# Turning the attention sinks by a float32r product, folding the older key block into the current one, and a new order of work

## The chip, the cores and the metric

The kernel runs on one core of a Trainium2 chip. The metric is the device time of one execution in microseconds (us); three runs of the kernel before took 260.81, 260.99 and 261.70 us, median 260.99. The engines of the core work side by side, each through its own list of instructions in order: TensorE (PE in the profile, its weight loads PEld), VectorE (DVE), ScalarE (ACT), GpSimd (POOL) and SyncE (SP), which issues most of the DMAs.

## The reference

Two layers, in float32, for B = 4, H = 8 heads, S = 768 positions, head width D = 64. First attention with a window and sinks, then a gated layer with a causal convolution of five taps:

```
scores = (q @ k.T) / sqrt(64)
keep   = (key < n_sink) | (0 <= query - key < window)      # n_sink 4, window 128
a      = exp(where(keep, scores, -1e9) - max);  a = a / (sum(a) + 1e-9)
x      = (a @ v)  laid out as [4, 768, 512]
gate   = 1 / (1 + exp(-conv5(x)));  out = ((gate * (x @ w_val)) @ w_out)
```

w_val, w_out and conv_w come as 64-bit numbers and are turned into pairs of float32r tiles in the kernel.

## The kernel before, in words

There are 24 steps s = (b, p, qd): batch b, a third p of the positions (256 queries), and a half qd of the head pairs. Two consecutive steps (qd = 0 and 1) make one block m = s // 2 of the second layer. `ORDER` is the whole plan: a list of 849 events, and each event (`s0.7` is `scores` of step 7, group 0) issues its instructions when its turn comes (line 685), so the order on every engine is written out by hand. All buffers rotate; a load or a product that needs a buffer in use waits for it.

The events of one step, with the line that issues their main instruction:

- `kq`, `vv` (234, 245): SyncE loads of k, q and v. `sv` (255) readies the sink rows of v on ScalarE and GpSimd.
- `s0`, `s1` (`scores`, 376): queries against keys, in float32. A query chunk c of 128 sees three key blocks of 64 (n = 200 columns with four sink columns behind each of the first two). Per group 16 products of a 64 x 32 tile and 168 columns, each as two instructions (L396). Window 128 over blocks of 64 means that for query r in its block the oldest key block counts at columns above r and the current one up to r, so one block can be folded into the other by a predicated copy (L401, VectorE): before, the current block is written over the oldest one where `low` is set, and the 132 columns [oldest, sinks, middle] are used. Then a maximum (L405), or for p = 0 mask and minimum in one (L410), where `mask` removes what lies ahead of the sequence.
- `e0`, `e1` (414): exp with its sum on ScalarE. `rec` (425): the reciprocal. `norm` (430): GpSimd multiplies the window part into `wx` (L436) and the sink part into `skb`, in three copies: the value (L440), its remainder (L444) and its rounding to float32r (L443).
- `tx` (449): 16 transposes of `wx` on TensorE; `px` (483) and `py` (491) mask and copy them into `wt`.
- `sk` (`sinks_t`, 462): the transpose of `skb` on TensorE (L464); `ts` (466): masks and rounds it into `skt`.
- `vl` (507): probabilities times values, float32 on 64 x 64 tiles (L518); `si` (522): the sinks' part, float32r (L526).
- `xc`, `xh`, `hd`, `xl` (531 to 550): x as float32 and as a high and a low float32r part. `c4`, `c0`, `c1` (552 to 562): the five taps. `th` (564): the gate, by tanh.
- per block, `v0` to `v3` (572): x @ w_val, 12 float32r products of 128 x 128 with 256 columns each (L581); `g`, `h`, `l` (597 to 610): gate times value and its two parts; `o0` to `o3` (612): times w_out, 6 products of 512 columns each (L634; the last block's second half as 12 of 256, L630). `t`, `d` (647, 658): copy and store.

The weights are decoded at the start (events `wv..`, `wo..`); there `woc` makes `wo_f` on GpSimd (L161) and `woe` uses it on TensorE (L184). `masks`, `signs`, `leads` and `blanks` (276 to 338) fill constants: `lead` holds what step 0 adds to its scores by a product, `plus` is the identity in float32r, `blanks` clears `skb`.

Of the kernel before, what the change touches and what calls it, by code (L numbers as in the profile page):

```python
# [42 lines left out]
s0.4 xh.1 vv.2 woe.1 c0.1 e1.3 rec.3 woa.3 th.0 vv.5 e0.4 xl.1 v0.0 v1.0 c1.1 y0.0 wob.3 woa.2 norm.3 g0.0  # L43
wod.3 h0.0 vl.2 wob.2 th.1 s1.4 e1.4 l0.0 v2.0 v3.0 woe.3 woe.2 y1.0 g1.0 vv.6 tx.3 px.3 si.2 xc.2 hd.2 wof.1
h1.0 s0.6 o2.0 o0.0 rec.4 xh.2 py.3 c4.2 c0.2 l1.0 wof.2 s0.5 c1.2 s1.6 kq.7 wod.2 e0.6 wof.3 o1.0 t0.0 o3.0
norm.4 sk.3 e0.5 vv.3 ts.3 t1.0 xl.2 vl.3 si.3 xh.3 xc.3 hd.3 xl.3 c4.3 sk.4 th.2 s1.5 ts.4 tx.4 sv.6 px.4
e1.5 kq.8 c0.3 scalars d0.0 py.4 rec.5 v0.1 v1.1 y0.1 c1.3 e1.6 rec.6 v2.1 norm.5 g0.1 th.3 h0.1 v3.1 vv.4
y1.1 vl.4 tx.5 d1.0 kq.9 si.4 g1.1 l0.1 px.5 s1.8 sk.5 hd.4 xc.4 ts.5 o0.1 h1.1 c4.4 o2.1 xh.4 c0.4 warm_up
c1.4 py.5 l1.1 e1.8 o3.1 t1.1 s0.7 s1.7 vl.5 xl.4 norm.6 kq.10 tx.6 e0.7 si.5 sk.6 py.6 px.6 ts.6 xc.5 xh.5
o1.1 hd.5 e1.7 xl.5 s0.9 rec.7 t0.1 s0.8 v0.2 c4.5 c0.5 v1.2 th.4 kq.12 g0.2 v2.2 c1.5 e0.9 norm.7 e0.8 rec.8  # L50
sk.7 h0.2 v3.2 l0.2 norm.8 tx.7 ts.7 th.5 g1.2 vl.6 py.7 si.6 px.7 hd.6 h1.2 xc.6 c4.6 l1.2 xh.6 xl.6 s1.9
s1.10 vv.7 c0.6 c1.6 o2.2 o0.2 vv.8 sv.7 e1.9 e1.10 o3.2 tx.8 rec.9 px.8 s0.12 vl.7 norm.9 kq.18 py.8 t1.2
si.7 xc.7 c4.7 s0.10 tx.9 d0.1 sk.8 hd.7 xh.7 xl.7 ts.8 th.6 c0.7 kq.11 e0.12 e0.10 o1.2 d1.2 v0.3 px.9 c1.7
vv.9 v1.3 g0.3 s1.12 py.9 t0.2 s0.11 rec.10 si.8 vl.8 xc.8 s1.11 kq.13 xh.8 h0.3 hd.8 d0.2 sk.9 c4.8 ts.9 l0.3
th.7 c0.8 c1.8 e0.11 norm.10 v2.3 v3.3 o2.3 vv.10 g1.3 s1.13 e1.11 tx.10 si.9 vl.9 px.10 h1.3 e1.12 rec.11
xc.9 l1.3 sk.10 xh.9 hd.9 ts.10 o3.3 c4.9 c0.9 py.10 norm.11 d1.1 kq.14 c1.9 o0.3 o1.3 e1.13 s1.18 tx.11 xl.9
t1.3 py.11 si.10 t0.3 px.11 vl.10 th.8 xc.10 rec.12 e1.18 d1.3 s0.18 s0.13 xl.8 vv.13 vv.12 vv.11 sk.11 th.9
v0.4 v1.4 ts.11 hd.10 v2.4 xh.10 d1.11 e0.18 v3.4 e0.13 c4.10 c0.10 c1.10 norm.12 kq.17 sv.13 kq.16 sv.12
tx.12 si.11 vl.11 py.12 g0.4 h0.4 g1.4 h1.4 hd.11 px.12 l0.4 s1.14 s0.14 sk.12 l1.4 xc.11 ts.12 rec.13 c4.11
c0.11 kq.15 e1.14 o2.4 o3.4 o0.4 norm.13 c1.11 e0.14 t1.4 th.10 o1.4 xl.10 tx.13 xh.11 si.12 px.13 t0.4 th.11  # L60
rec.14 py.13 vl.12 vv.18 xl.11 hd.12 xc.12 s1.15 c4.12 s0.15 xh.12 c0.12 xl.12 v0.5 v1.5 v2.5 d0.4 g0.5
norm.14 e1.15 sk.13 e0.15 vv.15 c1.12 v3.5 ts.13 g1.5 h0.5 tx.14 si.13 px.14 h1.5 s1.16 l0.5 py.14 vl.13
rec.15 hd.13 sk.14 l1.5 d1.4 xc.13 ts.14 c4.13 xh.13 o2.5 c0.13 o3.5 norm.15 s0.16 c1.13 xl.13 e1.16 s0.17
o0.5 o1.5 vv.14 e0.16 tx.15 t0.5 si.14 t1.5 th.12 vl.14 v0.6 px.15 rec.16 xc.14 hd.14 th.13 sk.15 ts.15 d0.5
v1.6 py.15 c4.14 v2.6 c0.14 e0.17 rec.18 v3.6 g0.6 norm.16 sk.16 c1.14 h0.6 kq.19 g1.6 norm.18 xh.14 h1.6
# [831 lines left out]
```

## Time and profile before

| | before |
|---|---|
| median of 3 runs | 260.99 us (260.81 to 261.70) |
| profiled execution | 260.89 us, span 259.1 us |
| TensorE busy | 251.7 us (97%), 3960 products |
| TensorE weight loads busy | 204.2 us (79%) |
| VectorE busy | 205.0 us (79%) |
| ScalarE busy | 187.1 us (72%) |
| GpSimd busy | 176.9 us (68%) |
| granted TensorE clock | 1.0 |

The span is the time from the first to the last instruction of the profile; 1.8 us of the execution lie outside it. A product's listed duration is that of its own passage through the array, and the next one starts before it is over, so the pace of TensorE is read from starts, not from durations. Idle time of an engine that others don't wait for costs nothing.

### The profile page before, as it was taken

Reading aid. Unit: us, or ns where it says so; the run is one execution under the profiler, and the core shown is the slowest. Engines: PE = TensorE matmul, PEld = TensorE weight load, DVE = VectorE, ACT = ScalarE, POOL = GpSimd, SP = SyncE. Lnnn points to the kernel's source line nnn. Section 1 sums busy time; section 2 is a strip of 40 time slices with the busy share of each in tenths; the row PEclk is TensorE's granted clock in tenths of the full one; section 3 lists DMA queues with packets and bytes.
Section 4 is the critical chain, followed back from the end, with each engine's and each line's share of the span. In section 5 each row is a group of like instructions: output and inputs, shape, how many; then the busy total and the mean of one; then the engine's idle time right before and its main releaser. Section 6 shows DMA issues by size and latency. Waiting matters only on the chain.

```text
span 259.1 us, 9951 instructions
## 1 busy us (share of the span) xinstructions
PE 251.7 (97%) x3960; PEld 204.2 (79%) x3964; DVE 205.0 (79%) x561; ACT 187.1 (72%) x692; POOL 176.9 (68%) x241
## 2 busy tenths in 40 slices
...
GB/s 211 378 333 329 140 259 61 129 159 199 4 106 217 82 82 231 324 4 251 168 156 144 3 65 242 83 233 165 3 104 221 91 4 9 177 83 0 3 61 114
DMA packets 27541, 36.45 MB, mean 141 GB/s; under 512 B 2272, under 2 KB 24032, under 8 KB 27488
## 3 DMA queue, kind: packets, MB, share of 16 engines
...
q14 instruction: 20, 0.16, 0.2%
...
## 4 chain that ended last, share of the span: by engine, by line
PE 84%; ACT 9%; DMA 2%; POOL 2%; DVE 1%; issue 1%
PE ac L581 26%; PE ac L634 22%; PE xv L518 12%; PE pr L396 10%; PE pr L456 5%; ACT w L421 4%; PE pr L634 3%; DMA raw<-in_w_val_dram 2%; PE xv L526 2%; PE ac L464 2%; ACT wv_p L141 1%; ACT wv_p L160 1%; ACT wvl L187 1%; PE ac L630 1%; PE pr L630 1%
## 5 line engine op out<-in xcount | busy, mean ns | idle before, releaser
L562 DVE SCALAR_TENSOR_TENSOR sg<-xv,cw,sg 128x256 f32<-128x256 f32 x192 | 77.8, 473 | 6.9 <-POOL sg L554 6.0
L436 POOL TENSOR_TENSOR wx<-w,sm 128x512 f32<-128x512 f32 x48 | 49.1, 1044 | 2.3 <-DVE sm L428 2.0
L421 ACT ACTIVATE w<-pr,ngm 128x132 f32<-128x132 f32 x136 | 48.5, 369 | 1.7
L581 PE MATMUL ac<-xh,wvh 128*128 128x256 f32 x192 | 48.3, 286 | 0.0
L581 PE MATMUL ac<-xh,wvl 128*128 128x256 f32 x192 | 47.2, 279 | 0.0
L554 POOL TENSOR_TENSOR sg<-xt,cw 128x512 f32<-128x512 f32 x24 | 25.4, 1060 | 29.1 <-ACT xt L533 28.8
L610 POOL TENSOR_TENSOR gl<-sg,gh 128x512 fp32r<-128x512 f32 x24 | 30.8, 1287 | 20.2 <-ACT gh L606 20.2
L581 PEld LDWEIGHTS ac<-xh,wvh 128*128 128x128 f32 x192 | 36.3, 189 | 1.5 <-issue 0.8
L581 PEld LDWEIGHTS ac<-xh,wvl 128*128 128x128 f32 x192 | 36.1, 188 | 0.3
L396 PE MATMUL pr<-k,q 64*32 64x168 f32 x1536 | 35.5, 307 | 0.2 <-DVE wt L487 0.2
L518 PE MATMUL xv<-wt,v 64*64 64x192 f32 (+2 forms) x1024 | 34.5, 278 | 0.2 <-ACT wt L495 0.2
L518 PEld LDWEIGHTS xv<-wt,v 64*64 64x64 f32 x1024 | 30.4, 133 | 5.1 <-issue 1.2
L634 PE MATMUL ac<-woh,gh 128*128 128x512 f32 x80 | 33.4, 417 | 0.0
L549 POOL TENSOR_TENSOR xl<-xt,xh 128x512 fp32r<-128x512 f32 x24 | 30.8, 1287 | 3.8 <-ACT xh L541 2.6
L634 PE MATMUL ac<-woh,gl 128*128 128x512 f32 x80 | 31.7, 396 | 0.0
L634 PE MATMUL ac<-wol,gh 128*128 128x512 f32 x80 | 31.6, 396 | 0.0
L581 PE MATMUL ac<-xl,wvh 128*128 128x256 f32 x192 | 30.2, 279 | 0.0
L396 PEld LDWEIGHTS pr<-k,q 64*32 64x32 f32 x1536 | 23.5, 106 | 7.6 <-issue 2.4
L401 DVE COPY_PREDICATED pr<-low,pr 128x256 f32<-128x256 uint8 x48 | 20.2, 422 | 11.3 <-PE pr L396 9.0
L421 ACT ACTIVATION_READ_ACCUMULATOR w<-pr,ngm 128x1 f32 x136 | 27.6, 203 | 0.0
L581 PEld LDWEIGHTS ac<-xl,wvh 128*128 128x128 f32 x192 | 25.8, 188 | 0.0
L405 DVE TENSOR_REDUCE ngm<-pr 128x4 f32<-128x528 f32 x34 | 24.0, 707 | 1.2
...
## 6 DMA issues: line engine op xcount, KB each, us to landing
...
```

Of the source, the lines that this page charges most:

```text
L396: nc.tensor.matmul(ss[e * QB:(e + 1) * QB, j, c * n + x0:c * n + x1], q[js, g, (4 * c + e) * QB:(4 * c + e + 1) * QB], k[js, g, (2 * c + e ...
L401: nc.vector.copy_predicated(sv[:, :, :, :D], low[:, None, None, :].to_broadcast([P, 2, 2, D]), sv[:, :, :, 2 * HB:])
L405: nc.vector.tensor_reduce(out=ngm[:, g], in_=sv[:, :, :, :PK], axis=mybir.AxisListType.X, op=ALU.max)
L421: nc.scalar.activation(out=w[:, g, j, c], in_=sx[:, j, c, :PK], func=AF.Exp, scale=0.125 if whole else -1.0, bias=ngm[:, g, j, c:c + 1], a ...
L436: nc.gpsimd.tensor_tensor(out=t[:, n].rearrange("p c h x -> p h c x"), in0=w[:, :, :, at], in1=sm.to_broadcast([P, 4, 2, D]), op=ALU.mult)
L518: nc.tensor.matmul(acc[o * D:(o + 1) * D, g, x0 + h * D:x0 + (h + a1 - a0 + 1) * D], v[js, g, n], t[js, n % 2, n // 2, g, a0:a1 + 1].rearr ...
L549: nc.gpsimd.tensor_tensor(out=half(xls, s, "xl", F32R), in0=xts[s], in1=half(xhs, s, "xh", F32R).bitcast(F32), op=ALU.subtract)
L554: nc.gpsimd.tensor_tensor(out=half(sg, s, "sg", F32), in0=xts[s], op=ALU.mult, in1=cw[:, g, KT - 1:].to_broadcast([P, 2, PQ]))
L562: nc.vector.scalar_tensor_tensor(out=g, in0=x, scalar=a, in1=g, op0=ALU.mult, op1=ALU.add)
L581: nc.tensor.matmul(acc[:, h], a[:, kc, cs], x[:, kc], start=(n == 0), stop=(n == 11))
L610: nc.gpsimd.tensor_tensor(out=gl, in0=g, in1=gh.bitcast(F32), op=ALU.subtract)
L634: nc.tensor.matmul(acc, a[:, kc, ts], x[:, kc], start=(kc + n == 0), stop=(kc + n == 5))
```

## The change

1. The sinks' transpose becomes a product of `skb` with the float32r identity `plus`; `skb` is a float32r tile, `normalise` first writes the sink part to a small float32 tile and rounds it into two places at once, and `blanks` clears `skb` by a multiplication.
2. In `scores` the oldest key block is folded into the current one (`high` in place of `low`), and the columns used are [middle, sinks, current]. Where the oldest block lies ahead of the sequence altogether (p = 0, c = 0), its 68 columns are neither computed (132 columns in place of 168 in each product) nor folded; `mask`, `lead` and the slices in `normalise` follow the new layout, and `lead` is partly copied from `mask`.
3. `ORDER` is the same set of 849 events; the first 116, up to and with `s0.4`, stand as before, and the others in a new order.

```diff
-        nc.vector.tensor_scalar(out=low, in0=d[:, :D], scalar1=0.0, scalar2=None, op0=ALU.is_ge)
+        nc.vector.tensor_scalar(out=high, in0=d[:, :D], scalar1=0.0, scalar2=None, op0=ALU.is_lt)
...
-        nc.gpsimd.memset(lead, 0.0)
-        nc.gpsimd.memset(lead[:, 0, :D], -BIG)
-        nc.gpsimd.memset(lead[lo, 0, HB:PK], -BIG)
-        nc.gpsimd.memset(lead[hi, 0, HB:HB + NSK], -BIG)
-        nc.gpsimd.memset(lead[lo, 0, 2 * HB:2 * HB + NSK], -BIG)
-        nc.gpsimd.memset(lead[lo, 1, :NSK], -BIG)
+        nc.gpsimd.memset(lead[:, 0, :HB], 0.0)
+        nc.gpsimd.memset(lead[:, 1], 0.0)
+        nc.gpsimd.memset(lead[:D, 1, :NSK], -BIG)
+        nc.vector.tensor_copy(out=lead[:, 0, HB:], in_=mask[:, 0])
         nc.gpsimd.tensor_copy(out=same, in_=ident)
-    skb = [cn.tile([P, P], F32, name=f"skb{n}") for n in range(2)]
+    skb = [cn.tile([P, P], F32R, name=f"skb{n}") for n in range(2)]
...
-            nc.gpsimd.memset(t, 0.0)
+            nc.gpsimd.tensor_scalar(out=t, in0=ident, scalar1=0.0, scalar2=None, op0=ALU.mult)
...
                     x0, x1 = (e % 2) * QB, n - QB + (e % 2) * QB
+                    if p + c == 0:
+                        x0, x1 = HB, n
...
-        nc.vector.copy_predicated(sv[:, :, :, :D], low[:, None, None, :].to_broadcast([P, 2, 2, D]),
-                                  sv[:, :, :, 2 * HB:])
+        c0 = 0 if p else 1
+        nc.vector.copy_predicated(sv[:, :, c0:, 2 * HB:], high[:, None, None, :].to_broadcast([P, 2, 2 - c0, D]),
+                                  sv[:, :, c0:, :D])
+        sv = sv[:, :, :, HB:]
...
-        sk = [skb[s % 2].rearrange("p (g k r) -> p k g r", g=2, r=NR)[:, n] for n in range(3)]
+        sk = skb[s % 2].rearrange("p (g k r) -> p k g r", g=2, r=NR)
...
-        nc.gpsimd.tensor_tensor(out=sk[0].rearrange("p g (h n) -> p g h n", n=NSK), in0=w[:, :, :, D:HB],
+        f = p2.tile([P, 2, NR], F32, name="skf", tag="skf")
+        nc.gpsimd.tensor_tensor(out=f.rearrange("p g (h n) -> p g h n", n=NSK), in0=w[:, :, :, D:HB],
                                 in1=sm.to_broadcast([P, 2, 4, NSK]), op=ALU.mult)
-        nc.gpsimd.tensor_scalar(out=sk[2].bitcast(F32R), in0=sk[0], scalar1=1.0, scalar2=None, op0=ALU.mult)
-        nc.gpsimd.tensor_tensor(out=sk[1], in0=sk[0], in1=sk[2], op=ALU.subtract)
+        nc.gpsimd.tensor_scalar(out=sk[:, 0:3:2], in0=f[:, None].to_broadcast([P, 2, 2, NR]), scalar1=1.0,
+                                scalar2=None, op0=ALU.mult)
+        nc.gpsimd.tensor_tensor(out=sk[:, 1], in0=f, in1=sk[:, 0].bitcast(F32), op=ALU.subtract)
...
-        nc.tensor.transpose(out=x[:, :P], in_=skb[s % 2], identity=ident)
+        nc.tensor.matmul(x[:, :P], skb[s % 2], plus, start=True, stop=True)
```

Of the order, TensorE's events from v0.0 on, before and after. A bar stands wherever the kind changes; `v` and `o` are one kind (full float32r products), and a `sk` is written behind what it follows, without a bar:

```
before
v0.0 v1.0 | vl.2 | s1.4 | v2.0 v3.0 | tx.3 | si.2 | s0.6 | o2.0 o0.0 | s0.5 s1.6 | o1.0 o3.0 sk.3 | vl.3 | si.3
sk.4 | s1.5 | tx.4 | v0.1 v1.1 v2.1 v3.1 | vl.4 | tx.5 | si.4 | s1.8 sk.5 | o0.1 o2.1 o3.1 | s0.7 s1.7 | vl.5 |
tx.6 | si.5 sk.6 | o1.1 | s0.9 s0.8 | v0.2 v1.2 v2.2 sk.7 v3.2 | tx.7 | vl.6 | si.6 | s1.9 s1.10 | o2.2 o0.2
o3.2 | tx.8 | s0.12 | vl.7 | si.7 | s0.10 | tx.9 sk.8 | o1.2 v0.3 v1.3 | s1.12 s0.11 | si.8 | vl.8 | s1.11 sk.9
| v2.3 v3.3 o2.3 | s1.13 | tx.10 | si.9 | vl.9 sk.10 | o3.3 o0.3 o1.3 | s1.18 | tx.11 | si.10 | vl.10 | s0.18
s0.13 sk.11 | v0.4 v1.4 v2.4 v3.4 | tx.12 | si.11 | vl.11 | s1.14 s0.14 sk.12 | o2.4 o3.4 o0.4 o1.4 | tx.13 |
si.12 | vl.12 | s1.15 s0.15 | v0.5 v1.5 v2.5 sk.13 v3.5 | tx.14 | si.13 | s1.16 | vl.13 sk.14 | o2.5 o3.5 |
s0.16 s0.17 | o0.5 o1.5 | tx.15 | si.14 | vl.14 | v0.6 sk.15 v1.6 v2.6 v3.6 sk.16 | s0.19 | tx.16 | si.15 |
vl.15 | s1.17 s1.19 | o0.6 o1.6 v0.7 v1.7 | tx.17 | tx.18 | si.16 | vl.16 | o2.6 sk.17 o3.6 v2.7 v3.7 | s1.20
s0.20 | si.17 sk.18 | o0.7 | vl.17 | s0.21 | o1.7 o2.7 sk.19 o3.7 | tx.19 | tx.20 | si.18 | vl.18 | s1.21 | v2.8
v0.8 v3.8 v1.8 | si.19 | vl.19 | s1.22 s0.22 sk.20 | o0.8 o1.8 v0.9 v1.9 | tx.21 | si.20 | vl.20 | s0.23 s1.23
sk.21 | o2.8 o3.8 v2.9 v3.9 | tx.22 | si.21 | vl.21 sk.22 | o0.9 o2.9 o3.9 o1.9 | tx.23 | si.22 | vl.22 sk.23 |
v0.10 v2.10 v1.10 v3.10 | si.23 | vl.23 | o0.10 o2.10 v0.11 v2.11 v1.11 v3.11 o1.10 o0.11 o1.11 o3.10 o2.11
o3.11
after
v0.0 v1.0 | vl.2 | si.2 | s1.4 s0.6 | v2.0 sk.3 v3.0 | tx.3 | s0.5 | o2.0 o0.0 o3.0 o1.0 | s1.6 s0.7 | vl.3 |
si.3 | tx.4 | s1.5 sk.4 | v0.1 v1.1 v2.1 v3.1 | s1.7 s1.8 | vl.4 | si.4 | tx.5 sk.5 | o2.1 o0.1 o1.1 | tx.6 |
vl.5 | si.5 | s0.9 s0.8 | o3.1 v0.2 v1.2 v2.2 sk.6 v3.2 sk.7 | tx.7 | vl.6 | si.6 | s1.9 s1.10 | o0.2 o2.2 o3.2
| s0.12 s0.10 | vl.7 | si.7 | tx.8 sk.8 | o1.2 v0.3 sk.9 v1.3 | tx.9 | si.8 | s1.12 | vl.8 | s1.11 s0.11 | v2.3
v3.3 o0.3 sk.10 | s0.13 | tx.10 | si.9 | vl.9 | s1.13 | o1.3 o2.3 o3.3 | tx.11 | si.10 | vl.10 | s0.18 s1.18 |
v0.4 sk.11 v1.4 v2.4 v3.4 | tx.12 | si.11 | vl.11 | s1.14 s0.14 sk.12 | o0.4 o1.4 o2.4 o3.4 sk.13 | tx.13 |
si.12 | vl.12 | s0.15 s1.15 | v0.5 v1.5 v2.5 v3.5 | tx.14 | si.13 sk.14 | vl.13 | s0.16 s1.16 | o2.5 o3.5 o0.5
o1.5 sk.15 | tx.15 | si.14 | vl.14 | s1.19 s0.17 | v0.6 v2.6 v1.6 v3.6 sk.16 | tx.16 | si.15 | vl.15 | s1.17
s0.19 | o0.6 o1.6 v0.7 v1.7 | tx.18 | tx.17 | si.16 | vl.16 | s1.20 sk.17 | v2.7 v3.7 o2.6 o3.6 sk.19 | s0.20
s0.21 | si.17 | vl.17 | o2.7 o3.7 o0.7 o1.7 sk.18 | tx.19 | tx.20 | si.18 | vl.18 | s1.21 | v0.8 v1.8 v2.8 v3.8
sk.20 | si.19 | vl.19 | s0.22 s1.22 | o0.8 o1.8 v0.9 v1.9 | tx.21 | si.20 | vl.20 | s1.23 s0.23 sk.21 | o2.8
o3.8 v2.9 v3.9 sk.22 | tx.22 | si.21 | vl.21 | o2.9 o3.9 o0.9 o1.9 sk.23 | tx.23 | si.22 | vl.22 | v0.10 v1.10
v2.10 v3.10 | si.23 | vl.23 | o2.10 o0.10 v0.11 v1.11 v2.11 v3.11 o1.10 o0.11 o1.11 o3.10 o2.11 o3.11
```

The other engines' events move with these. SyncE's loads and stores, `scalars` (the load of n_sink and window) and `flag` (their comparison on VectorE, now the last but two events) are moved too.

## Rows read from the trace of the kernel before

**Rows 1.** The page: busy time by engine, and the chain that ended last.

```profile
PE 251.7 (97%) x3960; PEld 204.2 (79%) x3964; DVE 205.0 (79%) x561; ACT 187.1 (72%) x692; POOL 176.9 (68%) x241
...
PE 84%; ACT 9%; DMA 2%; POOL 2%; DVE 1%; issue 1%
```

**Rows 2.** Busy time by stretch: stretch, its length, engines' busy us (instructions), clock, DMA.

```profile
38.00:146.00 108.00, 108.00 (x1915) 91.66 (x1914) 95.92 (x277) 88.23 (x346) 80.60 (x104) 1.00 0.46 142
146.00:255.20 109.20, 109.09 (x1576) 94.12 (x1572) 77.49 (x191) 65.82 (x228) 68.23 (x84) 1.00 0.30 96
```

**Rows 3.** TensorE in order of time, 42 to 46 us: start, length, instruction.

```profile
42.20 0.80 PE L396 MATMUL pr<-k,q 64*32 64x168 f32 x32
42.93 0.38 PE L581 MATMUL ac<-xh,wvh 128*128 128x256 f32 x1
43.15 0.28 PE L581 MATMUL ac<-xh,wvl 128*128 128x256 f32 x1
...
45.39 0.63 PE L581 MATMUL ac<-xl,wvh 128*128 128x256 f32 x4
45.95 0.71 PE L456 MATMUL pr<-ident,wx 64*128 64x64 f32 x16
```

**Rows 4.** TensorE in order of time, two calls of scores at 50 us.

```profile
50.50 1.37 PE L396 MATMUL pr<-k,q 64*32 64x168 f32 x64
51.80 0.50 PE L634 MATMUL ac<-woh,gh 128*128 128x512 f32 x1
52.14 0.40 PE L634 MATMUL ac<-wol,gh 128*128 128x512 f32 x1
```

**Rows 5.** TensorE in order of time: values of a p = 0 step and another.

```profile
136.97 1.21 PE L518 MATMUL xv<-wt,v 64*64 64x192 f32 x32
138.11 1.39 PE L396 MATMUL pr<-k,q 64*32 64x168 f32 x64
...
156.23 1.55 PE L518 MATMUL xv<-wt,v 64*64 64x64 f32 x48
157.71 0.38 PE L581 MATMUL ac<-xh,wvh 128*128 128x256 f32 x1
```

**Rows 6.** TensorE in order of time around three of the sinks' transposes.

```profile
67.22 0.33 PE L464 MATMUL ac<-ident,skb 128*128 128x128 f32 x1
...
67.62 0.40 PE L634 MATMUL ac<-wol,gh 128*128 128x512 f32 x1
...
143.75 0.27 PE L464 MATMUL ac<-ident,skb 128*128 128x128 f32 x1
...
143.98 0.28 PE L581 MATMUL ac<-xh,wvl 128*128 128x256 f32 x1
144.10 0.28 PE L581 MATMUL ac<-xh,wvh 128*128 128x256 f32 x1
...
163.11 0.64 PE L581 MATMUL ac<-xl,wvh 128*128 128x256 f32 x4
...
163.79 0.80 PE L396 MATMUL pr<-k,q 64*32 64x168 f32 x32
```

**Rows 7.** Groups by line and shape: busy us, mean ns of one, idle before.

```profile
L581 PEld LDWEIGHTS ac<-xh,wvl 128*128 128x128 f32 x192 | 36.1, 188 | 0.3
...
L518 PEld LDWEIGHTS xv<-wt,v 64*64 64x64 f32 x1024 | 30.4, 133 | 5.1 <-issue 1.2 <-ACT wt L495 0.5 <-PE ac L634 0.3
...
L396 PEld LDWEIGHTS pr<-k,q 64*32 64x32 f32 x1536 | 23.5, 106 | 7.6 <-issue 2.4 <-DVE wt L487 0.8 <-ACT w L421 0.7
...
L443 POOL TENSOR_SCALAR skb<-skb 128x32 fp32r<-128x32 f32 x24 | 8.1, 338 | 2.1
```

**Rows 8.** GpSimd and TensorE in order of time ahead of 38 us.

```profile
14.25 2.51 POOL L161 TENSOR_TENSOR wv_f<-wv_e,wv_p 128x512 fp32r<-128x512 f32 x2 [3.90 <-ACT wv_p L160]
...
32.50 1.29 POOL L264 TENSOR_TENSOR vh<-vs,vh 16x128 fp32r<-16x128 f32 x2 [0.25 <-POOL skb L444]
...
37.49 0.50 PE L184 MATMUL ac<-wo_f,plus 128*128 128x512 f32 x1 [0.68 <-POOL wo_f L161]
```

More of the change, by code (lines that the diff above doesn't have):

```diff
@@ L42 @@
 wvf.3 sv.1 tx.2 py.2 px.2 s1.3 xl.0 sk.1 ts.1 wod.1 wvf.2 kq.4 vl.1 si.1 xc.1 c4.1 sk.2 ts.2 kq.6 hd.1 woc.1
[L43 to L65, printed above, removed]
-s0.19 kq.22 tx.16 l0.6 py.16 si.15 px.16 vl.15 xc.15 xl.14 s1.17 vv.16 vv.19 d1.5 s1.19 xh.15 ts.16 hd.15 o0.6
@@ L77 @@
-o1.9 tx.23 c0.21 th.20 vv.23 d0.8 t0.9 t1.9 c1.21 py.23 si.22 vl.22 xc.22 sk.23 flag hd.22 xh.22 ts.23 v0.10
-px.23 c4.22 c0.22 v2.10 v1.10 c1.22 g0.10 v3.10 d1.6 h0.10 th.21 th.22 l0.10 xl.22 si.23 vl.23 o0.10 g1.10
-xh.23 xc.23 xl.23 hd.23 d0.9 h1.10 c4.23 c0.23 c1.23 o2.10 l1.10 v0.11 v2.11 v1.11 v3.11 th.23 g0.11 h0.11
-o1.10 g1.11 d1.9 h1.11 l0.11 o0.11 l1.11 t0.10 o1.11 o3.10 t0.11 d0.10 t1.10 d0.11 d1.10 o2.11 o3.11 t1.11
+s0.4 vv.3 xh.1 e1.3 c0.1 th.0 vv.2 xl.1 woe.1 c1.1 rec.3 v0.0 woa.2 wob.2 v1.0 woe.2 e0.4 y0.0 vl.2 th.1 wof.1
```

64 lines of the change are left out of this document (45 added, 19 removed).

## The prediction

> **What bounds the kernel now.** I read four views, from coarse to fine. The page's first lines [rows 1] give the first suspect: TensorE has work for 97% of the span and makes up 84% of the chain that ended last. The reader should not stop there, since a share over the whole span can hide a start with another limit. So the second view cuts the span into stretches [rows 2]. From 38 us on TensorE is busy 108.00 of 108 us and then 109.09 of 109.2 us; VectorE, the next in load, has 95.92 of the same 108 us and 77.49 of the second stretch. From 38 us to the end the time is therefore the sum of what TensorE has to do, and a change is worth there what it takes from that sum, as long as no other engine gets late. The first 38 us are another matter: the last thing that TensorE waits for before its long run is GpSimd's `wo_f`, 0.68 us at 37.49 us [rows 8]. The third view is TensorE in order of time. There the start of one product and the start of the next is what counts: the listed durations overlap, and busy time alone would not show what a change of kind costs. The fourth, the groups of instructions by shape, gives the weight loads.
>
> From the third view come three prices. First, a change between float32 products on small tiles and the full float32r products (`v`, `o`; I call a run of them a V stretch). Inside a stretch products of 256 columns start every 0.12 us (143.98 to 144.10) [rows 6], but the first after scores takes 0.22 us (42.93 to 43.15), 0.10 more, and after the last four, which should take 4 x 0.117 = 0.47 us, the transposes start 0.56 us later (45.39 to 45.95), 0.09 more [rows 3]. A V stretch costs 0.19 us beside its products. Second, one call of scores takes 0.73 us (42.20 to 42.93) [rows 3] and two in a row 1.30 us (50.50 to 51.80) [rows 4]: 0.57 us each and 0.16 us for each stretch of them. Third, the sinks' transpose, whose cost depends on its neighbours: between two V products 143.75 to 143.98 is 0.23 us for it and one product, so 0.11 us; between scores and V 67.22 to 67.62 is 0.40 us [rows 6] where scores followed by V have 0.34 (51.80 to 52.14) [rows 4], so 0.06 us; behind V and ahead of scores 163.11 to 163.79 is 0.68 us [rows 6] against 0.56 [rows 3], so 0.12 us.
>
> **The change part by part.**
>
> The order. I walked both lists of TensorE's events from v0.0 on. The events are the same; only the neighbours differ. The old order has 28 V stretches (a `sk` inside one doesn't end it, since it is priced by itself), the new one 24: 4 x 0.19 = 0.76 us less. It has 26 stretches of scores, the new one 23: 3 x 0.16 = 0.48 us less. All of it is TensorE's own time in the part where nothing hides it. Sum of the order: -1.2 us.
>
> Narrower scores. For p = 0 and c = 0 the 16 instructions of a call stream 132 columns, not 168. Does time follow columns here? In the values it does: the p = 0 step streams 16 x 192 + 8 x 128 + 8 x 64 = 4608 instruction columns in 1.14 us (136.97 to 138.11), the others 6144 in 1.48 us (156.23 to 157.71) [rows 5]; three quarters of the columns take 0.77 of the time, so columns and not instructions set it. A call of scores has 32 x 168 = 5376 instruction columns in 0.57 us; 16 x 36 = 576 fewer are 0.06 us. There are 8 steps with p = 0, two calls each; steps 0 and 1 lie ahead of 38 us, where TensorE waits for others anyway. 12 x 0.06 = 0.73 us less; the bounds are 0 and this.
> The Trainium skill (TensorE: Matmul & The Clock Gate, section "Wait — 56ns, not 53.3ns?") says that starts never come closer than about 25 ns, however few the columns. The trace differs: 64 instructions of scores in 1.30 us [rows 4] are 20 ns each, fill and drain included. By the page this term would be nothing and the sum -1.0 us; that is rival C.
>
> The sinks' product. A transpose of a float32 tile becomes a float32r product of 128 columns, 21 of them behind 38 us. No row has a float32r product of fewer than 256 columns, so it is bounded from both sides. From below: the pace of `v`, 0.117 us for 256 columns [rows 6], gives 0.06 us for 128. From above: float32 scores cost 0.57 us for 16 products of 168 columns, eight side by side, which is 0.57 x 8 / (16 x 168) = 1.7 ns a column, nearly four times the 0.46 ns of `v`; at that rate 128 columns are 0.22 us. I take the lower end for streaming, by the nearest row, the same operand type on the same full array, but add the load of the next weights. Loads of 32, 64 and 128 columns last 106, 133 and 188 ns [rows 7], 0.85 ns a column, so 128 columns occupy the load path some 0.11 us (an estimate from these three), which a 256-column product just covers and a 128-column one doesn't. So a `sk` that is followed by V costs 0.12 us, one that is followed by small tiles 0.06. New order: 4 between V and V and 6 between small tiles and V, 10 x 0.12; 10 behind V and ahead of small tiles, 10 x 0.06; sk.14 between `si` and `vl`, taken at 0.12: 1.9 us. Old order: 5 between V and V x 0.11, 13 ahead of V x 0.06, 2 behind V x 0.12, one between small tiles at 0.12: 1.7 us. Difference +0.2 us, with ends -0.4 (all at 0.06: 1.3) and +2.9 (all at 0.22: 4.6).
> The Trainium skill (FP8 and Floating Point Precision, section "TensorE Precision Notes") gives true float32 four passes and lets reduced float32 be read once; it makes no exception for few columns. By it the upper end would not occur; no row decides it.
>
> GpSimd and the start. In `normalise` the rounding now writes 64 columns, not 32; an L443 takes 338 ns in the mean [rows 7], so the extra lies between nothing and 0.34 us a step, and I take 0.1. Behind 38 us GpSimd is busy 80.60 of 108 us [rows 2] and 24 x 0.1 us disappear in its gaps; without that cover `wx` would come late and tx behind it, up to the 2.4 us. Ahead of 38 us GpSimd is what TensorE waits for last, with three normalises before `wo_f`. But it stands 0.25 us still before the second `vh` pair [rows 8], where it needs ScalarE's `vh`, so of 0.3 us some 0.1 gets through; with 0.34 each it would be 0.8. The dearer `blanks` fall into GpSimd's 3.90 us of waiting ahead of 14.25 us [rows 8]; `leads` has fewer instructions on GpSimd and one copy more on VectorE, ahead of work that waits for the first weights. The half as wide predicated copy of p = 0 takes load from VectorE, which TensorE doesn't wait for: nothing.
>
> What is moved past queues. Loads of k, q and v keep three buffers each. Walking SyncE's list with the release of each buffer, the tightest load behind the changed point, kq.13, can be issued some 7 us ahead of its first product (an estimate with the prices above). Stores move later (d0.2 behind t0.4) but never hold more than the three output buffers. The flag's small VectorE instructions go from step 22 to the very end, behind g1.11, where five `o` events of 1.4 us each are still to run on TensorE; hidden, and at the end by their own length if VectorE were that late. `scalars` moves too and nothing but the flag reads it.
>
> Sum: -0.76 - 0.48 - 0.73 + 0.2 + 0.1 = -1.7 us. The profiled execution took 260.89 us, its span 259.1, 1.8 us outside of it, which I leave as it is. 260.89 - 1.7 = 259.2 us. The median of the three runs is 260.99, 0.1 above the profiled one and less than I can tell apart; the forecast is 259.2 us.
>
> **The rivals.**
>
> A: the short product is dear. With 128 columns the float32r product runs at the float32 rate of 1.7 ns a column, 0.22 us in each of 21 places. For it: every float32r row has 256 columns or more, and nothing shows a shorter one to be fast. Against it: the operand type, the array and the moving matrix (`plus`) are those of products that run at 0.46 ns a column. The term is +2.9 in place of +0.2: 260.89 + 1.0 = 261.9 us, slower. It decides from 0.17 us a product on: (1.9 saved elsewhere + 1.7 of the old ones) / 21.
>
> B: the new order loses cover. VectorE is 89% busy from 38 to 146 us [rows 2], and every engine works its own list in order. Two places have less between producer and consumer than before: v0.3 stands behind tx.8, sk.8 and o1.2, some 2.1 us after si.7 (0.5, 0.1, six products of 512 columns 1.4, one change 0.1; in the old order s0.10 as well, 2.8), and si.18 stands behind sk.18 with only two transposes, 1.0 us, between. If several such waits cost 0.3 to 0.5 us each, 1.5 us are given back: about 260.7 us, no change. For it: the margin was bought by TensorE never waiting in the old order. Against it: the shortest margins from scores to transposes and from transposes to values are about as long as before.
>
> C: the narrower scores pay nothing, since instructions and not columns set their pace: 259.2 + 0.73 = 259.9 us.
>
> **How the numbers follow.** Forecast 0.55, A 0.17, B 0.18, C 0.10. A measurement of this kernel tells 0.3%, 0.8 us, from no change. The forecast and most of C are faster (under 260.2); most of B and the rest of C lie within; A and the worst of B are slower (above 261.8): 0.65, 0.17, 0.18. The range goes from 257.8 (the sinks' product at its lower end, -0.6 more, and some tenths of TensorE's present waits gone) to 261.9 (rival A). The forecast's own range is 257.8 to 260.2.
>
> **What would show it.** In the trace after, TensorE should still be busy for all but a few tenths from 38 us on, with 24 and 23 stretches. A call of scores of p = 0 behind 38 us should start its successor 0.67 us later, 0.73 in the others. The sinks' product should add 0.06 to 0.12 us to the starts around it; 0.2 or more is rival A. The product at 37.49 us that waits for `wo_f` should move by less than 0.3 us. Gaps of TensorE behind `xh` or `skt` would be rival B. I am wrong if the span falls by over 3 us, or if TensorE's work falls as reckoned and the span does not.

## The result, and the profile after

The kernel after takes 262.96 us (median of six runs, 262.75 to 263.16) beside 261.11 for the kernel before in the same session: ratio 1.0072, 95% interval 1.006 to 1.0083. It is slower, and outside the forecast's range. The profiled execution took 263.02 us with a span of 261.2, so 2.1 us over the [rows 1, 2] kernel's 259.1.

The page of the kernel after, its lines on TensorE's busy time and on the chain that ended last:

```profile
PE 251.1 (96%) x3964; PEld 205.2 (79%) x3964; DVE 205.6 (79%) x562; ACT 187.5 (72%) x692; POOL 181.2 (69%) x238
...
PE 77%; ACT 10%; DVE 6%; DMA 2%; POOL 1%; issue 1%; DVEq 0%
```

TensorE is listed as busy for a little less time than in [rows 1], but its share of the chain fell from 84 to 77%, VectorE's rose from 1 to 6%. So the time went into waiting. The stretches show where (columns as in [rows 2]):

```profile
38.00:146.00 108.00, 105.93 (x1889) 90.56 (x1889) 95.47 (x275) 87.00 (x342) 80.65 (x102) 1.00 0.47 147
146.00:255.20 109.20, 109.20 (x1590) 95.34 (x1589) 78.77 (x193) 66.99 (x232) 71.50 (x86) 1.00 0.28 88
```

TensorE, without a gap in the first stretch before, now stands idle in it for 2.07 us. Its waits behind 38 us (line, releaser: us in total, times, longest):

```profile
PE ac L637 <- POOL gl L613: 0.9, 1, 0.9
PE pr L459 <- ACT w L422: 0.7, 1, 0.7
PE xv L521 <- PE pr L459: 0.2, 1, 0.2
PE xv L521 <- PE pr L395: 0.2, 1, 0.2
```

The first two, 1.67 us with a few hundredths beside them, lie between 46.9 and 53.9 us: tx.3 waits for exponentials, and step 0's output product for the lower half of its gated values, `l1.0`. TensorE's own sequence makes the bill of the span: v0.0 starts at 37.82 us in place of 37.83; from there to the last product's end there is 216.59 us of work, the time in which a product is listed as running, in place of 217.26 (-0.67); 2.07 us idle in place of none; and from that end to the end of the span 4.76 us in place of 4.02 (+0.74). Together +2.1 us.

This work is not free of waiting. In step 0's output product the products start 0.23 us apart, but each is listed for 0.40 us; so a wait counts as idle only from where the listed time of the product before it ends. And the first product behind a wait takes 0.34 us to its successor:

```profile
49.37 0.40 PE L637 MATMUL ac<-wol,gh 128*128 128x512 f32 x1
49.81 0.50 PE L637 MATMUL ac<-woh,gl 128*128 128x512 f32 x1
50.14 0.40 PE L637 MATMUL ac<-woh,gh 128*128 128x512 f32 x1
...
52.47 0.40 PE L637 MATMUL ac<-wol,gh 128*128 128x512 f32 x1
53.81 0.50 PE L637 MATMUL ac<-woh,gl 128*128 128x512 f32 x1 [0.95 <-POOL gl L613]
54.15 0.40 PE L637 MATMUL ac<-woh,gh 128*128 128x512 f32 x1
```

The waits for `l0.0` (to 49.81) and `l1.0` (to 53.81) cost 0.3 and 1.2 us by the starts, where 0.04 and 0.95 are listed as idle. So the -0.67 is too small a figure for what the change took from the products themselves; the experiments come back to it.

Behind `l1.0` stands GpSimd's list. In the kernel before:

```profile
43.38 1.34 POOL L610 TENSOR_TENSOR gl<-sg,gh 128x512 fp32r<-128x512 f32 x1 [0.83 <-ACT gh L606]
...
48.94 1.29 POOL L610 TENSOR_TENSOR gl<-sg,gh 128x512 fp32r<-128x512 f32 x1
50.20 2.52 POOL L173 TENSOR_TENSOR wol<-wo_e,wo_p 128x512 fp32r<-128x512 f32 x2
```

and in the kernel after, where `l1.0` is the last line:

```profile
40.11 2.57 POOL L437 TENSOR_TENSOR wx<-w,sm 128x512 f32<-128x512 f32 x2 [1.44 <-DVE sm L429]
...
44.15 1.74 POOL L173 TENSOR_TENSOR wol<-wo_e,wo_p 128x512 fp32r<-128x512 f32 x1
...
48.20 1.55 POOL L613 TENSOR_TENSOR gl<-sg,gh 128x512 fp32r<-128x512 f32 x1 [1.31 <-ACT gh L609]
50.84 1.68 POOL L173 TENSOR_TENSOR wol<-wo_e,wo_p 128x512 fp32r<-128x512 f32 x1 [1.09 <-DVE wo_p L169]
52.49 1.26 POOL L613 TENSOR_TENSOR gl<-sg,gh 128x512 fp32r<-128x512 f32 x1
```

`l1.0` starts 3.55 us later. The last decode instructions of two tiles of the output weights (L173, `wof.2` and `wof.3`) now stand ahead of it, step 3's `wx` starts late because the reciprocal that it needs was moved behind both convolutions (38.50 to 39.83 us), and VectorE, which feeds all of it, is late as well. VectorE in the same time:

```profile
40.35 1.42 DVE L146 SCALAR_TENSOR_TENSOR wo_t<-wo_p,wo_t 128x512 int32<-128x512 int32 x1
41.80 1.15 DVE L152 TENSOR_SCALAR wo_e<-wo_t 128x512 int32<-128x512 int32 x1
...
43.99 0.74 DVE L603 SCALAR_TENSOR_TENSOR sg<-sg,vc 128x512 f32<-128x512 f32 x1
```

The last line is g0.0, at 41.75 us before. The two decode instructions ahead of it run beside `wx`; the experiments show what they take alone.

The end of the kernel, SyncE's stores:

```profile
255.57 0.33 SPq L648 DMA_DIRECT2D out_dram<-osb  x1
255.94 1.54 SPq L664 DMA_DIRECT2D out_dram<-osb  x1
257.59 0.38 SPq L648 DMA_DIRECT2D out_dram<-osb  x1
```

d1.10 (L664) now comes next to last in SyncE's list and holds the queue for 1.54 us; the last piece's store, whose copy ended at 256.90, is issued at 257.59.

### The profile page after: what moved, and what is told of

The parts are those of the page before. It is cut to its first block, busy times and chain, and to the rows that moved or that the text cites. A ratio compares the mean times of both kernels' runs of the same rounds, so it can differ in the third digit from the quotient of the medians.

```text
span 261.2 us, 9941 instructions
## 1 busy us (share of the span) xinstructions
PE 251.1 (96%) x3964; PEld 205.2 (79%) x3964; DVE 205.6 (79%) x562; ACT 187.5 (72%) x692; POOL 181.2 (69%) x238
## 4 chain that ended last, share of the span: by engine, by line
PE 77%; ACT 10%; DVE 6%; DMA 2%; POOL 1%; issue 1%; DVEq 0%
PE ac L584 24%; PE ac L637 21%; PE xv L521 11%; PE pr L395 9%; PE pr L459 5%; ACT w L422 4%; PE pr L637 3%; PE xv L529 2%; DMA raw<-in_w_val_dram 2%; DVE sg L565 2%; PE ac L467 1%; DVE wo_t L146 1%; ACT wvl L187 1%; ACT wv_p L141 1%; DVE wo_f L167 1%
## 5 line engine op out<-in xcount | busy, mean ns | idle before, releaser
L437 POOL TENSOR_TENSOR wx<-w,sm 128x512 f32<-128x512 f32 x48 | 49.7, 1057 | 7.0 <-DVE sm L429 6.8
L395 PE MATMUL pr<-k,q 64*32 64x168 f32 (+1 forms) x1536 | 34.0, 302 | 0.3 <-DVE wt L490 0.2
L637 PE MATMUL ac<-woh,gh 128*128 128x512 f32 x80 | 32.8, 410 | 0.0
L395 PEld LDWEIGHTS pr<-k,q 64*32 64x32 f32 x1536 | 22.8, 105 | 6.1 <-issue 1.9
L401 DVE COPY_PREDICATED pr<-high,pr 128x256 f32<-128x256 uint8 (+1 forms) x48 | 18.2, 379 | 10.0 <-PE pr L395 9.8
```

The lines of the kernel that those rows point to most:

```text
L395: nc.tensor.matmul(ss[e * QB:(e + 1) * QB, j, c * n + x0:c * n + x1], q[js, g, (4 * c + e) * QB:(4 * c + e + 1) * QB], k[js, g, (2 * c + e ...
L401: nc.vector.copy_predicated(sv[:, :, c0:, 2 * HB:], high[:, None, None, :].to_broadcast([P, 2, 2 - c0, D]), sv[:, :, c0:, :D])
L437: nc.gpsimd.tensor_tensor(out=t[:, n].rearrange("p c h x -> p h c x"), in0=w[:, :, :, at], in1=sm.to_broadcast([P, 4, 2, D]), op=ALU.mult)
L637: nc.tensor.matmul(acc, a[:, kc, ts], x[:, kc], start=(kc + n == 0), stop=(kc + n == 5))
```

## The experiments

Times are medians beside the kernel before on the same chip. Where TensorE's work is given, it is the time from v0.0 to its last product's end less its listed idle time, from the one profiled execution of each.

**Order and operations apart.** The first run has the new operations in the old order, the second the old operations in the new one.

```diff
 # e1_old_order: the kernel after
-ORDER = (new)
+ORDER = (that of before)
 # e2_order_only: the kernel before
-ORDER = (old)
+ORDER = (that of after)
```

> Both edits of the operations (float32r product for the sinks, older block folded into the current one), the order of before. Theory 1, the loss is in the new order (VectorE late between 40 and 56 us, 2.2 us, and a store moved to the very end, 0.7 us): the narrower scores give 0.7 back and the sinks' product costs 0.3 to 0.4 in the old places, so 260.6 to 260.9 us, slightly under before. Theory 2, the new operations are what costs: 262.5 us or more.

> The new order alone, with the operations of before. Theory 1: the early wait and the late store stay, and the 0.7 us of the narrower scores is lost, so 263.3 to 264.2 us. Theory 2: about as before or faster, 259.9 to 261.2 us.

Measured: 261.45 us, ratio 1.0009 (0.9998 to 1.002), and 264.39 us, 1.0118 (1.0103 to 1.0132), beside 261.19. The loss is the order's, as theory 1 has it, but both times lie above its ranges: the new operations do not gain what they were expected to in the old order, and the order costs 3.2 us with the old operations and some 1.6 with the new.

**One operation at a time**, in the old order, and the narrower scores in the new one.

```diff
 # e7_fold_only: e1_old_order
-        nc.tensor.matmul(x[:, :P], skb[s % 2], plus, start=True, stop=True)
+        nc.tensor.transpose(out=x[:, :P], in_=skb[s % 2], identity=ident)
 #   (and skb, blanks and normalise as before)
 # e8_product_only: the kernel before, with all of these the other way round
 # e13_fold_new_order: e7_fold_only with ORDER = (that of after)
```

> The old order with one of the two new parts alone: the older key blocks folded into the current one (narrower scores); the sinks' transposes as before. If the narrower scores pay what was forecast (0.06 us for each of 12 calls) and nothing takes it back: 260.4 to 260.7 us beside 261.19 for the kernel before, TensorE's scores 0.6 to 0.7 us less in sum. If the gain is put off behind other engines: 261.0 to 261.3 us, with new idle time on TensorE.

> The old order with the other part alone: the sinks turned by a float32r product; scores as before. Forecast's price (0.06 to 0.12 us for each of 24): 0.2 us over the kernel before, 261.3 to 261.5 us. If the product, with its change of data type, costs more than its own columns, as the two parts together in the old order make likely (they gained 0.5 us in the scores and were 0.26 us slower): 261.6 to 262.0 us, with TensorE busy throughout, so that the loss is in its own work.

> The new order with the narrower scores and the old transposes of the sinks, so the kernel after without the float32r product. If the parts add up as they did in the old order (product alone +0.49 us): 262.4 to 262.6 us, half a microsecond under the kernel after. If the product is what lets the new order put a sink inside a stretch of float32r products without breaking it (new order alone 264.39 us, narrower scores alone -0.52): 263.7 to 264.1 us, a microsecond over the kernel after.

Measured: narrower scores alone 260.77 us, 0.9984 (0.9971 to 0.9998); product alone 261.78, 1.0016 (1.0006 to 1.0026), both beside 261.29; narrower scores in the new order 263.37, 1.0079 (1.0061 to 1.0098), beside 261.24. The last lies between its two expectations. The product costs half a microsecond in the old order; in the new one it gains 0.2 us by the two ratios (inside their intervals, so the times alone don't show it) and 0.37 of TensorE's work:

| TensorE's work, us (idle) | old order | new order |
|---|---|---|
| old operations | 217.26 (0.00) | 217.78 (2.23) |
| narrower scores | 216.95 (0.02) | 216.96 (1.98) |
| product | 217.78 (0.02) | not run |
| both | 217.29 (0.06) | 216.59 (2.07) |

The idle time belongs to the new order whatever the operations are. The work seems to fall through the order only with both operations, by 0.70 us, and to rise by 0.5 with the old ones; but it holds the unlisted part of the waits, of which the old order has hardly any. An estimate without them: take for each event of TensorE the time from its first start to the next event's, and price it at the median of all such events between the same kinds of neighbours in the 17 traces (as neighbours `v` and `o` are one kind; narrow and wide scores are two kinds of event, and so are the two ways to turn the sinks).

| TensorE's events at their usual price, us (what the execution took beyond it, listed idle time included) | old order | new order |
|---|---|---|
| old operations | 217.1 (0.2) | 215.9 (4.1) |
| narrower scores | 216.6 (0.4) | 215.4 (3.5) |
| product | 217.6 (0.2) | not run |
| both | 217.0 (0.3) | 215.2 (3.5) |

So the new order does take time from TensorE's products, 1.2 us with the old operations and 1.9 with both, and the whole change takes 1.9 (1.3 to 2.0 when the lowest or the lower quartile stands for the median, or `v` and `o` are told apart). Its waits cost 3.1 to 3.9 us more than what the old order with the same operations loses, and some 2 of them are listed as idle.

**The end.**

```diff
 # e3_store_back: the kernel after
-... d0.11 o2.11 o3.11 flag d1.10 t1.11
+... d0.11 d1.10 o2.11 o3.11 t1.11      (flag ahead of v0.10)
```

> The changed kernel with two events moved: the store d1.10 ahead of o2.11 again, as in the old order, and flag ahead of v0.10. Theory 1: the last store no longer stands behind d1.10 in the queue of SyncE, 0.7 us less, 262.2 to 262.4 us, and the time from the end of TensorE to the end of the span is 4.0 us as before, not 4.7. Rival: that time is set by something else (the flag, the landing), and the median stays at 262.9 to 263.1.

Measured: 262.67 us, 1.0053 (1.004 to 1.0066). From TensorE's last product to the end of the span it is 4.04 us, as before the change. By the ratios it gives back 0.5 us, the profiled spans differ by 0.6: the right place, less than the 0.7 expected. That stretch varies by itself: it is 4.47 to 4.85 us in the six traces with the store next to last (mean 4.71) and 3.99 to 4.54 in the seven with it moved back (mean 4.28), so some 0.4 us is the store's.

**The start: five attempts to mend it in place.** First only the reciprocal, then only the decode; then both with GpSimd's parts; then the scores that the new order moved up.

```diff
 # e5_rec3: the kernel after
-... woe.1 c1.1 rec.3 v0.0 ...
+... woe.1 rec.3 c1.1 v0.0 ...
 # e10_decode_later: the kernel after
-... v0.0 woa.2 wob.2 v1.0 woe.2 ... g0.0 s1.4 xc.2 s0.6 e1.4 ...
+... v0.0 woa.2 v1.0 ... g0.0 s1.4 xc.2 s0.6 e1.4 wob.2 woe.2 ...
 # e12_queues: e5_rec3 and e3_store_back, and
-... h0.0 wob.3 sk.3 woe.3 v3.0 wof.2 ... g1.0 ... l0.0 py.3 wof.3 ... l1.0 ...
+... h0.0 sk.3 v3.0 ... g1.0 wob.3 woe.3 ... l0.0 wof.2 py.3 ... l1.0 wof.3 ...
 # e15_s06_later: e5_rec3 and e3_store_back, and
-... s1.4 xc.2 s0.6 e1.4 ... tx.3 s0.5 ... o0.0 e0.6 ...
+... s1.4 xc.2 e1.4 ... tx.3 s0.6 ... o0.0 s0.5 e0.6 e0.5 ...
 # e16_split_o: e5_rec3 and e3_store_back, and
-... o0.0 e0.6 o3.0 o1.0 c1.2 s1.6 ...
+... o0.0 s1.6 e0.6 o3.0 o1.0 c1.2 ...
```

> The kernel after, with one VectorE instruction moved: step 3's reciprocal goes back between the two groups of convolution products (c0.1 and c1.1), 1.3 us earlier. Theory 1 (the late reciprocal puts step 3's products on GpSimd beside VectorE's weight decode, and the two engines slow each other): GpSimd's first wx of step 3 starts at 38.8 us instead of 40.1 and lasts some 2.0 us, the decode's L146 falls from 1.42 to about 0.7 us, g0.0 comes at about 42.6 us instead of 44.0, TensorE's idle time between 38 and 56 us falls from 1.67 to 0.5 to 1.0 us, and the time is 261.9 to 262.4 us. Theory 2 (what counts is that all of the decode of one tile of the output weights stands ahead of g0.0 and of the next scores on VectorE): TensorE's idle time there stays above 1.3 us and the time within 0.3 us of 262.9.

> The kernel after, with two events of the decode of output weights 2 (wob.2 and woe.2, on VectorE 1.42 + 1.15 + 0.47 + 0.69 us in the kernel after) moved behind the exponentials e1.4, so that g0.0 and the reductions of s1.4 stand ahead of them; the reciprocal stays late. Theory 2 (position of the decode): g0.0 comes at 41 to 42 us, TensorE's idle time between 38 and 56 us falls below 0.6 us, the time is 261.2 to 261.8 us. Theory 1 alone (late reciprocal, two engines slowing each other): the products of step 3 still start at 40.1 us, tx.3 still waits about 0.5 us, idle time about 1 us, 262.1 to 262.5 us. If both add up, this run and the one with the earlier reciprocal each take a part.

> The kernel after with what stood in the queues ahead of step 0's gated values put right: step 3's reciprocal between c0.1 and c1.1, VectorE's decode of output weights 3 (wob.3, woe.3) behind g1.0, GpSimd's wof.2 behind l0.0 and wof.3 behind l1.0, and at the end the store d1.10 ahead of o2.11 and the flag ahead of v0.10. Theory (the loss is instructions waiting in order on VectorE and GpSimd ahead of what TensorE needs): l1.0 starts at 49 to 50 us (52.5 in the kernel after), TensorE's idle time between 38 and 56 us falls from 1.67 to under 0.6 us, and the time is 261.1 to 261.7 us. Rival (any early gain is given back at the next place that waits, as the version with the old start gave back half): idle time between 56 and 80 us grows by as much as is saved, and the time stays at 262.3 us or more.

> The kernel after with one merged stretch of scores undone: s0.6 goes from behind s1.4 to the place of s0.5 (behind tx.3), and s0.5 between o0.0 and o3.0, as in the old order; step 3's reciprocal between c0.1 and c1.1, and the store d1.10 and the flag moved back as well. Theory (the scores of s0.6, moved up, put 1.5 us of VectorE work ahead of the decode and of g1.0, and that is what makes l1.0 late for the second half of step 0's output product): g1.0 and l1.0 come 1.2 to 1.8 us earlier than with the reciprocal alone (l1.0 at 50.3 to 50.9 us instead of 52.1), the output product no longer waits for l1.0, TensorE's idle time between 38 and 56 us is under 0.6 us, 261.2 to 261.8 us. Rival (the decode's own length beside GpSimd decides): l1.0 stays behind 51.8 us, idle time over 1 us, 262.0 to 262.4 us.

> The kernel after with the stretch of step 0's output product split again: s1.6 between o0.0 and o3.0, so that 0.7 us of scores lie ahead of the first product that needs l1.0; reciprocal, store and flag moved back as in the version beside it, s0.6 left where the new order has it. If l1.0's lateness is all that TensorE waits for there, the wait of 0.9 us falls to 0.2 to 0.4 us and the split costs 0.3 us: 262.0 to 262.3 us. If the scores find no free pair of PSUM banks there, the wait only changes its name: 262.4 us or more.

Measured: 262.61 us, 1.0048 (1.003 to 1.0066); 267.33, 1.0227 (1.0201 to 1.0253); 266.06, 1.0189 (1.0167 to 1.0211); 263.82, 1.0091 (1.0076 to 1.0105); 265.17, 1.0138 (1.0114 to 1.0161). The first did what theory 1 said to the decode (L146 at 0.69 us, g0.0 at 43.67) but only a fifth of the early idle time went: 1.34 us are left, and idle time and median are what theory 2 said. The other four are slower than the kernel after.

e10_decode_later is the instructive one. VectorE in it, the decode of weights 2 and then of weights 3 (its lines are numbered three lower than in the kernel after, L143 for L146):

```profile
46.12 0.69 DVE L143 SCALAR_TENSOR_TENSOR wo_t<-wo_p,wo_t 128x512 int32<-128x512 int32 x1
46.85 0.43 DVE L149 TENSOR_SCALAR wo_e<-wo_t 128x512 int32<-128x512 int32 x1
...
48.71 1.64 DVE L143 SCALAR_TENSOR_TENSOR wo_t<-wo_p,wo_t 128x512 int32<-128x512 int32 x1
50.45 1.08 DVE L149 TENSOR_SCALAR wo_e<-wo_t 128x512 int32<-128x512 int32 x1
51.45 1.48 DVE L164 TENSOR_SCALAR wo_f<-raw 128x512 int32<-128x512 int32 x1
```

and GpSimd beside it:

```profile
48.41 1.38 POOL L170 TENSOR_TENSOR wol<-wo_e,wo_p 128x512 fp32r<-128x512 f32 x1 [4.83 <-DVE wo_p L166]
49.76 1.49 POOL L554 TENSOR_TENSOR sg<-xt,cw 128x512 f32<-128x512 f32 x1
51.21 1.44 POOL L610 TENSOR_TENSOR gl<-sg,gh 128x512 fp32r<-128x512 f32 x1
```

The reader is to see two things. While GpSimd stood still (4.83 us, to 48.41) the decode took 0.69 and 0.43 us; beside GpSimd's work the same instructions took 1.64 and 1.08. And GpSimd stood still because `wof.2` was at the head of its list and its input had been moved back: `sg` and step 0's `l0.0` queued behind it, and l0.0 came at 51.21 us in place of 48.20. TensorE in that kernel:

```profile
48.59 0.40 PE L634 MATMUL ac<-wol,gh 128*128 128x512 f32 x1
52.70 0.80 PE L634 MATMUL ac<-woh,gl 128*128 128x512 f32 x1 [3.72 <-POOL gl L610]
53.30 0.63 PE L634 MATMUL ac<-woh,gh 128*128 128x512 f32 x1
53.73 0.63 PE L634 MATMUL ac<-wol,gh 128*128 128x512 f32 x1
...
58.40 0.40 PE L634 MATMUL ac<-wol,gh 128*128 128x512 f32 x1
58.63 0.40 PE L634 MATMUL ac<-woh,gl 128*128 128x512 f32 x1
```

After 3.72 us of standing still the products start every 0.43 us instead of 0.23, for some five microseconds. The stretches of the same kernel say why (columns as in [rows 2]; the granted clock is the third number from the end):

```profile
50.00:52.00 2.00, 0.00 (x0) 0.00 (x0) 1.90 (x3) 0.00 (x0) 2.00 (x2) 0.75 0.00 0
52.00:54.00 2.00, 1.29 (x3) 1.10 (x4) 1.97 (x3) 0.00 (x0) 0.91 (x2) 0.50 0.00 0
54.00:56.00 2.00, 2.00 (x6) 1.52 (x6) 1.97 (x5) 1.67 (x6) 2.00 (x2) 0.50 0.00 0
```

TensorE's clock fell to half, 1.2 GHz, and its work is 218.62 us where the same products take 216.59 in the kernel after. So this wait cost 3.7 us and some 2 us more.

e12_queues waits at the same place for `wof.3` (1.95 us), whose decode now comes late on VectorE, and for `l1.0` (0.8); there the clock falls too (0.70 and 0.50 from 56 to 60 us). In e15_s06_later `l1.0` is at 51.85 us, only 0.25 earlier than with the reciprocal alone, though 1.5 us of VectorE work went from ahead of it: the decode moved up beside GpSimd's work and grew (two of its instructions took 1.41 and 1.65 us, 0.69 each alone). The rival holds. TensorE's longest wait there, and the two longest in e16_split_o, have other names:

```profile
PE pr L392 <- DVE sg L562: 1.7, 1, 1.7
```

```profile
PE pr L392 <- DVE sg L562: 2.2, 1, 2.2
PE xv L518 <- DMA v<-in_vt_dram: 1.0, 1, 1.0
```

The scores put between the output products wait behind VectorE's list; behind the 1.7 us the clock falls to 0.50 (56 to 58 us), behind the 2.2 us it falls again (means of 0.59 and 0.56 over 56 to 58 and 58 to 60 us). The 1.0 us for a load of v, at 41 us, is in this execution alone and isn't explained.

**The old start, cut at two places.** e4 keeps the old order up to step 0's last store, e14 mends the two waits seen in it, e17 cuts where the two orders have done nearly the same work.

```diff
 # e4_old_start: the kernel after; ORDER = old up to t1.0, then the rest as in the new
 #   (vv.7 behind vl.5)
 # e14_mended: e4_old_start with the end of e3_store_back, and
-... o1.0 t0.0 o3.0 norm.4 sk.3 e0.5 ...    ... o1.1 tx.6 ... o3.1 ...
+... o1.0 e0.5 t0.0 o3.0 norm.4 sk.3 ...    ... o1.1 o3.1 tx.6 ...
 # e17_late_seam: the kernel after with the end of e3_store_back; ORDER = old up to
 #   o0.2 (behind o2.2), then the rest as in the new
 # e18_best: e17_late_seam, and
+        if s < 8: nc.tensor.transpose(out=x[:, :P], in_=skb[s % 2].bitcast(F32), identity=ident)
+        else:     nc.tensor.matmul(x[:, :P], skb[s % 2], plus, start=True, stop=True)
```

> The changed operations, the old order up to t1.0 (some 55 us), and behind it what is left in the new order (the load vv.7 later, for its buffer). Theory 1: the 2.2 us of TensorE's waits between 45 and 54 us are gone, the late store stays: 260.5 to 261.2 us. Theory 2: as the changed kernel, 262.7 to 263.2 us. If the waits are only put off by the new order's later part, between the two.

> All new operations, the old order up to t1.0 and the new one from there on, with the waits that this version showed mended: e0.5 ahead of the copy t0.0 on ScalarE (the copy waited 1.5 us for TensorE with the exponentials queued behind it), o3.1 moved up behind o1.1 (step 5's values waited 0.4 us at 74.8 us for VectorE's convolution), d1.10 ahead of o2.11 and the flag ahead of v0.10. If these queues are all that is left between the version and its own work: TensorE idle under 0.3 us from 38 us on, 260.2 to 260.7 us, faster than the kernel before and at least level with the narrower scores alone (260.77). If the merged stretches pay nothing: 261.0 us or more without idle time.

> All new operations; the old order up to step 2's first output product (o2.2, some 88 us; there the two orders have done the same work but for three to four events), the new order from there on, with the store d1.10 and the flag moved back. From that product to TensorE's end the kernel after takes 166.72 us and the new operations in the old order 167.43, before that the kernel after stood idle for 2.07 us. Theory (the new order's loss lies wholly ahead of 88 us, and its merged stretches pay 0.7 us behind it): 260.6 to 260.9 us, no idle time on TensorE over 0.2 us. Rival (the merges only pay because the work behind them was late): 261.3 us or more, with new idle time behind 88 us.

> The version beside it with the sinks of steps 0 to 7, those in the old order, turned by the old transposes, and the float32r product from step 8 on, where the new order puts it inside float32r stretches. Up to the first output product of step 2 the old transposes took 0.19 us less than the product (49.73 us with narrower scores alone, 49.92 with both): 260.4 to 260.7 us, the fastest so far by 0.1 to 0.3 us. If the product's price is the same in both orders: no difference from the version beside it beyond 0.1 us.

Measured: e4 262.15 us, 1.0034 (1.0021 to 1.0047); e14 263.07, 1.0067 (1.0047 to 1.0087); e17 260.90, 0.9988 (0.9979 to 0.9997); e18 260.92, 0.9986 (0.9974 to 0.9998). e4 still stands idle for 1.38 us: at its seam the scores wait 0.9 us, because ScalarE's copy t0.0 waits 1.5 us for TensorE with the exponentials of s0.5 behind it. Mending its two places in e14 brought two new waits, 0.7 and 0.4 us, and 1.63 us of idle time in all.

e17 is the answer. Its stretches ahead of 88 us and behind:

```profile
38.00:88.00 50.00, 49.94 (x897) 42.45 (x896) 43.36 (x121) 43.00 (x162) 38.17 (x47) 1.00 0.38 120
88.00:255.00 167.00, 166.79 (x2593) 144.46 (x2590) 129.30 (x347) 112.06 (x414) 112.66 (x142) 1.00 0.39 119
```

TensorE's work is 216.67 us, as little as in the kernel after, and its idle time 0.16. So the new order loses its time on TensorE ahead of 88 us, and its merged stretches pay behind it as they stand. Which of the events moved ahead of 88 us makes the waits is not shown. e17, e18 and the narrower scores alone (260.77) beat the kernel before by 0.1 to 0.2%, by intervals that end just below 1, and among the three nothing can be told apart; e18's expected 0.2 us did not come.

## Why the prediction was wrong

The step that failed is the condition in its first part: a change is worth what it takes from TensorE's sum "as long as no other engine gets late". [Rows 2] had the warning, VectorE at 95.92 of 108 us, and that mean hid that from 38 to 56 us VectorE is busy for 17.62 of 18 us, in both kernels. Rival B had the mechanism but placed it at v0.3 and si.18, where nothing is listed as waiting (TensorE isn't listed idle behind 76 us), and priced it at 1.5 us. It struck mostly where the output weights are still being decoded: 1.67 us of listed idle time there and 0.40 more at 68 and 76 us, 3.3 us in all by the estimate above (3.5 less the 0.2 of the kernel before). The sum itself was about right: the prediction's four terms of TensorE's products come to -1.8 us, the estimate to -1.9 (-1.3 to -2.0). The lateness had no term in it, nor had the end of the kernel.

Point by point, the forecast beside the runs:

- Order, -1.24 us, and sinks' product, +0.2: the second sets the product in its new places against the transposes in their old ones, so the two are to be read together, forecast at -1.0. From narrower scores in the old order to both operations in the new one the estimate has -1.4 (216.6 to 215.2). Listed work has -0.36, since the new order's waits are in it.
- Narrower scores, -0.73 us: -0.5 by the estimate in either order. Listed work has -0.31 in the old order and -0.82 in the new one, and single stretches make the difference: in e7_fold_only s1.12 and s0.11 take 1.39 us (1.30 before, 1.24 for the same calls in e1_old_order), and in e2_order_only s0.18 and s1.18 take 1.56, which take 1.23 in the kernel after. What held them up isn't listed. The price of a call was right where it stands alone, 0.73 to 0.67 us (e7_fold_only, 92.62 to 93.35 before):

```profile
92.67 0.74 PE L392 MATMUL pr<-k,q 64*32 64x132 f32 x32
93.34 0.39 PE L516 MATMUL xv<-wt,v 64*64 64x192 f32 x4
```

  It was mostly right, too, where a call opens a stretch of two (0.59 to 0.53 us); a call that closes one mostly gains 0.015 (0.71 to 0.69), and why isn't settled. Eight of the twelve calls behind 38 us stand alone or open a stretch, in either order. A stretch with one of each, s1.6 and s0.7, takes 1.30 us in e2_order_only (56.47 to 57.77) and 1.22 in the kernel after (56.35 to 57.57). Rival C is out.
- The price of one sinks' product: rival A is out. In the kernel after one between V and V takes 84.64 to 84.92 with one product, so 0.16 us (0.12 forecast), and one behind V 86.21 to 86.36, 0.15 with V's exit of 0.09, so 0.06 (as forecast):

```profile
84.64 0.28 PE L467 MATMUL ac<-plus,skb 128*128 128x128 f32 x1
84.75 0.33 PE L584 MATMUL ac<-xh,wvh 128*128 128x256 f32 x1
84.92 0.28 PE L584 MATMUL ac<-xh,wvl 128*128 128x256 f32 x1
...
86.21 0.22 PE L467 MATMUL ac<-plus,skb 128*128 128x128 f32 x1
86.36 0.46 PE L459 MATMUL pr<-ident,wx 64*128 64x64 f32 x7
```

  Against the transposes in the same places the product is +0.5 us in the old order, where 13 stand ahead of V, and -0.3 in the new one (both by the estimate). The prediction's own prices by place have +0.7 and -0.2, so its prices held roughly, and the sign does hang on the order.
- GpSimd and the start, +0.1 us: nothing. The product that waits for `wo_f` moved from 37.49 to 37.47 us, though the wider rounding takes 370 ns in the median.
- Moved past queues: the loads were right. The stores were passed over because they hold no buffer; the very end, where the last store's place in SyncE's list is the time, was not looked at: +0.74 us in the profiled run, of which moving the store gave back 0.4 to 0.5.

With the measured terms the sum is -1.9 us of TensorE's products and +3.3 of its waits (both by the estimate; -0.7 and +2.1 as listed), and +0.7 at the end. Not settled is whether any small move would mend the waits of the new order ahead of 56 us: none of those tried did.
